# Logits and slot sums behind the v matmuls, one load in the first cycle, and two weight conversions moved into the attention

## The chip, the cores and the metric

The program runs on one core of a Trainium2 chip. A core has five engines with an instruction queue each: TensorE (PE in the profile) multiplies matrices into PSUM, VectorE (DVE), ScalarE (ACT) and GpSimd (POOL) do elementwise work, and SyncE (SP) issues the DMAs here. Each queue runs in order; a wait at its head holds everything behind it. The metric is the device time of one execution in microseconds (us).

## The reference

Attention in chunks of 64 feeds a soft mixture of experts, whose output feeds a gated feed-forward stage.

```
scores = scale * q_c @ k_c.T;  attn = softmax(scores);  x = attn @ v_c     # 8 x 8 heads, 576 tokens, chunks of 64
logits = x @ phi                                                           # x: 4608 x 512, phi: 512 x 32
d = softmax(logits, over tokens);  slot_input = d.T @ x                    # 32 slots, 4 for each of 8 experts
slot_out[e] = relu(slot_input[e] @ w1[e]) @ w2[e]                          # w1: 512 x 1024, w2: 1024 x 512
x2 = softmax(logits, over slots) @ slot_out
g = x2 @ w_gate;  out = (g * sigmoid(g) * (x2 @ w_val)) @ w_out            # 1536 wide
```

The weights w_gate, w_val and w_out arrive as float64. [...]

## The kernel before, in words

The order of the instructions on each engine is that of the program text; nothing reorders them.

**Attention.** The 4608 tokens are 36 tiles of 128. A loop of 19 cycles (k = 0 to 18) handles two tiles per cycle, with the steps of different pairs overlapped. In cycle k, with a = k - 1: logits or the slot sum of an earlier group of four tiles (`emit_logits` in cycles with odd a, `emit_si` in those with even a), the v matmuls of pair a (`emit_pv`, L370, then the reciprocals and the x product on DVE, L386 to L393), the transposes of the scores (`emit_pt`, L356, with the exponential on ACT, L358), the scores of the next pair (`emit_scores`, L333, then max and subtraction on DVE, L341 and L343, tile ssb), POOL's spread of the next v tiles (`spread_v`, L323), the transposes of x (`emit_xt`, L406), and in cycles with odd a the transpose of e (`emit_et`, L458, with its copy on ACT, L460). A slot sum (L471) reads e and four tiles of x. The pool of x has four buffers of one pair each, and a slot sum reads the oldest two.

**Loads.** All loads go through SP's queue. Four q/k tiles and four v tiles are in flight in rings (L290, L293). After each step `pump(n)` takes up to n entries from a list of the loads that later stages need: the float64 data of the first gate and value halves (`load_gv0`), scratch space (`alloc_tmp`, no DMA), then the experts' weights, 32 loads of one MB (`load_w`, L88), with the second gate and value halves (`load_gv0` 1) three entries before their end, then the raw float64 chunks. Each entry needs one of 16 slots; in the attention no slot comes free, and from its end four more are there (in the space of the rings).

**Conversions.** A unit of float64 data passes through `conv_a` (ACT L190, DVE L191 and L192), `conv_b` (ACT L199, DVE L200) and `conv_c` (DVE L205, a product on POOL). `conv_step` moves each unit under way one step on and may start the next; `conv_pos` counts finished units. The first four units are the gate and value halves 0 and 1.

**Experts.** Sixteen steps (w1 or w2 of one expert, L626 and L671), n = 0 to 15, are written with pieces of other work between: steps of the softmax over slots (`emit_c1` on DVE and ACT, `emit_c2` with L709 on PE, at the positions `C_AT`) and conversion steps at the positions `CV_AT`. The last w2 is followed by the scaled slot outputs and the feed-forward stage, which fills the second half of the program.

Of the kernel before, what the change touches and what calls it, by code (L numbers as in the profile page):

```python
# [21 lines left out]
NSP = 9  # L22
RESV = 6
R0 = 7.4
CV_AT = (2, 3, 4, 5, 14)
LATE = 3
C_AT = (3, 4, 5, 6, 7, 9, 10, 11, 12)
RATE = 0.38
# [5 lines left out]
def tile_attn_softmoe_swiglu(  # L34
# [18 lines left out]
    NG = NT // 512  # L53
# [92 lines left out]
    def pump(n=99):  # L146
        while n and lq:
            f, *a = lq[-1]
            if slots[0] > (0 if f in (load_w, load_gv0, alloc_tmp) or a[-1] == 0 else min(resv[0], RESV)):
                f(*a, wp)  # L150
                slots[0] -= 1
                owner[f.__name__, tuple(a)] = 0
            elif slots[1] and f is load_w:
                f(*a, wx[0])
                slots[1] -= 1
                owner[f.__name__, tuple(a)] = 1
            else:
                return
            lq.pop()
            n -= 1  # L160
# [93 lines left out]
    def conv_step(start=True):  # L254
        for k, f in (("d", conv_d), ("c", conv_c), ("b", conv_b)):
            if stage[k]:
                f()
        if start and conv_ready():
            conv_a()

    def conv_busy():
        return bool(stage["b"] or stage["c"] or stage["d"])

    def conv_pos():
        n = len(conv_q) + sum(len(x) for x in stage.values())
        return 6 * NSC - n

    def conv_until(n):
        while conv_pos() < n:
            assert conv_busy() or conv_ready()  # L270
            conv_step(6 * NSC - len(conv_q) < n)

    with tc.manual_schedule():
# [89 lines left out]
        def emit_pv(p):  # L363
            xa = ps_x.tile([128, 2, 512], F32, tag="xa", name="xa_ps")
            xb = ps_x.tile([128, 512], F32, tag="xb", name="xb_ps")
            banks = [xa[:, 0], xa[:, 1], xb]
            for n in range(8):
                i, j = 2 * p + n // 4, n % 4
                for cc in range(2):
                    nc.tensor.matmul(  # L370
                        out=banks[n // 3][64 * cc:64 * cc + 64, (n % 3) * 2 * VW:(n % 3 + 1) * 2 * VW],
                        lhsT=pt_t[i][:, j, 64 * cc:64 * cc + 64],
                        rhs=v_bd[i % NV][:, :, cc, j, :],
                        start=True, stop=True,
                    )
                if j == 3:
                    pt_t.pop(i)
                    if i + NV < NTILE:
                        load_v(i + NV)
            x = xp.tile([128, 2, 512], F32, tag="x", name="x_sb")  # L380
            rec = sm.tile([128, 16, 1], F32, tag="rec", name="rec", bufs=2)
            av = xa[:, :, 0:6 * VW].rearrange("p b (h d) -> p b h d", d=VW)
            bv = xb[:, 0:4 * VW].rearrange("p (h d) -> p h d", d=VW)
            ra, rb = rec[:, 0:12].rearrange("p (b h) o -> p b h o", b=2), rec[:, 12:16]
            xv = x.rearrange("p t (h d) -> p (t h) d", d=D)
            nc.vector.tensor_scalar(out=ra, in0=av[:, :, :, D:VW], scalar1=1e-9, scalar2=None, op0=ALU.add)  # L386
            nc.vector.tensor_scalar(out=rb, in0=bv[:, :, D:VW], scalar1=1e-9, scalar2=None, op0=ALU.add)
            nc.vector.reciprocal(out=rec, in_=rec)
            nc.vector.tensor_tensor(
                out=xv[:, 0:12].rearrange("p (b h) d -> p b h d", b=2), in0=av[:, :, :, 0:D],  # L390
                in1=ra.to_broadcast([128, 2, 6, D]), op=ALU.mult,
            )
            nc.vector.tensor_tensor(  # L393
                out=xv[:, 12:16], in0=bv[:, :, 0:D], in1=rb.to_broadcast([128, 4, D]), op=ALU.mult
            )
            x_t[2 * p], x_t[2 * p + 1] = x[:, 0], x[:, 1]
# [3 lines left out]
        def emit_xt(i):  # L400
            xt = xtp.tile([128, 4, 128], F32, tag="xt", name="xt")
            n = 4 if i < NTILE - 1 else 2
            for j0 in range(0, 4, n):
                ps = ps_t.tile([128, 4, 128], F32, tag="t", name="xt_ps")
                for j in range(j0, j0 + n):
                    nc.tensor.transpose(ps[:, j - j0, :], x_t[i][:, j * 128:(j + 1) * 128], ident)  # L406
                if j0 == 0:
                    nc.scalar.activation(out=xt[:, 0:n], in_=ps[:, 0:n], func=ACTF.Copy)  # L408
                else:
                    nc.vector.tensor_copy(out=xt[:, j0:j0 + n], in_=ps[:, 0:n])  # L410
            xt_t[i] = xt
# [55 lines left out]
        def emit_si(g, mid=None):  # L467
            e = e_t.pop(g)
            ps = ps_t.tile([128, 512], F32, tag="t", name="si_ps")
            for jt in range(4):  # L470
                nc.tensor.matmul(  # L471
                    out=ps[32 * jt:32 * jt + 32, :],
                    lhsT=e[:, 32 * jt:32 * jt + 32],
                    rhs=x_t.pop(4 * g + jt),
                    start=True, stop=True,
                    tile_position=(0, 32 * jt),
                )
            if mid:
                mid()
            if g:  # L480
                be = beta_t.pop(g)
                n = DM // 2 if g == NG - 1 else DM
                for o in range(0, DM, n):
                    nc.vector.scalar_tensor_tensor(
                        out=acc[:, o:o + n], in0=acc[:, o:o + n], scalar=be, in1=ps[:, o:o + n],
                        op0=ALU.mult, op1=ALU.add,
                    )
            else:
                nc.vector.tensor_copy(out=acc, in_=ps)
# [43 lines left out]
        NP = NTILE // 2  # L533
        for k in range(NP + 1):
            a = k - 1
            if a >= 3 and a % 2:
                emit_logits((a - 3) // 2)
            elif a >= 4:
                emit_si((a - 4) // 2)
            if a >= 0:  # L540
                emit_pv(a)
            if k < NP:
                emit_pt(2 * k)
                emit_pt(2 * k + 1)
            if k + 1 < NP:
                emit_scores(k + 1)
                spread_v(2 * k + 2)
                spread_v(2 * k + 3)
            if a >= 1:
                emit_xt(2 * a - 2)  # L550
                emit_xt(2 * a - 1)
            if a >= 3 and a % 2:
                emit_et((a - 3) // 2)
            if k == 0:
                pump(4)
            elif k % 4 != 3:
                pump(1)
        emit_si(NG - 2)
        emit_xt(NTILE - 2)
        emit_xt(NTILE - 1)  # L560
        emit_logits(NG - 1)
        pr.close()
        wx[0] = pa.enter_context(tc.tile_pool(name="wx", bufs=NWX, side="right", reuse_waits="tile"))
# [422 lines left out]
```

## Time and profile before

| | us |
|---|---|
| median of 3 runs | 582.43 (581.38 to 583.82) |
| profiled execution | 582.74 |
| its span, first to last instruction | 579.9 |
| PE busy | 533.8 (92%) |
| DVE busy | 409.4 (71%) |
| ACT busy | 262.1 (45%) |
| POOL busy | 253.1 (44%) |
| slot outputs complete (last L671) | 204.3 |

The span is the part of an execution that the trace shows; the rest lies around it. A busy share is a mean over stages. In the trace a row can carry in brackets how long the engine was idle before it and what released it. "GB/s" is what the 16 DMA engines moved, "DMA share" how busy they were, "PEclk" the clock granted to TensorE as a share of the full one.

### The profile page before, as it was taken

The numbers are of one execution on the slowest core, as the hardware profiler recorded it, in microseconds if no ns is written. First come the engines' busy times: TensorE is split into PE (matmuls) and PEld (weight loads), VectorE is DVE, ScalarE is ACT, GpSimd is POOL, SyncE is SP. The second block draws the span as 40 slices with busy tenths as digits, with TensorE's granted clock in tenths as the row PEclk, the third lists the DMA queues.
The fourth block names the chain that finished last, engine by engine and source line by source line (L and its number), as shares of the span: only waits on it lengthen the run. The fifth ranks groups of instructions, "written<-read, shape, count | busy, mean of one in ns | idle before, by whom it ended". The sixth has DMA issues, their size and how long they took to land.

```text
span 579.9 us, 11070 instructions
## 1 busy us (share of the span) xinstructions
PE 533.8 (92%) x4405; PEld 416.6 (72%) x4405; DVE 409.4 (71%) x679; ACT 262.1 (45%) x508; POOL 253.1 (44%) x252
## 2 busy tenths in 40 slices
PE   7599999998972977999999999999999999999997
PEld 6477777775421465888888887887888788888885
DVE  5557777774643579998888887997989763443464
ACT  1233333334323466766666555554645443333331
POOL 3133424331010226566656665764666463434432
PEclk9889999999995998999999999999999999999999
DMA  8999999976999930010120222024000000032245
GB/s 325 400 393 364 320 360 347 359 255 229 338 387 381 393 113 1 5 68 6 69 73 1 72 73 73 1 73 145 1 1 0 2 1 1 5 122 91 73 173 189
DMA packets 37970, 91.09 MB, mean 157 GB/s; under 512 B 3104, under 2 KB 5152, under 8 KB 37920
## 3 DMA queue, kind: packets, MB, share of 16 engines
q1 hardware_dynamic: 37920, 90.40, 43.0%
q8 instruction: 34, 0.56, 0.4%
q14 instruction: 16, 0.13, 0.1%
HBM read 80.95 MB, written 9.44 MB: 156 GB/s over the span
## 4 chain that ended last, share of the span: by engine, by line
PE 78%; DMA 8%; DVE 6%; ACT 4%; issue 1%; POOL 1%; SPq 1%; DVEq 0%; ACTq 0%; POOLq 0%
PE o L867 17%; PE o L868 16%; PE o L869 16%; PE xa_ps L370 4%; PE v_ps L823 4%; PE g_ps L823 4%; DMA vbd<-in_v_dram 4%; ACT xt L408 3%; PE pt_ps L356 3%; PE s_ps L333 3%; DMA raw<-in_moe_w_gate_dram 2%; DMA raw<-in_moe_w_val_dram 2%; PE xt_ps L406 2%; PE lt_ps L424 2%; PE si_ps L471 2%; PE gg_ps L804 2%
## 5 line engine op out<-in xcount | busy, mean ns | idle before, releaser
L836 POOL TENSOR_TENSOR lo_sb<-s_sb,hi_sb 128x512 fp32r<-128x512 f32 x106 | 140.4, 1325 | 134.1 <-ACT hi_sb L835 130.7
L867 PE MATMUL o<-whl,hi_sb 128*128 128x512 f32 x428 | 168.0, 393 | 2.5 <-DVE part L876 2.5
L869 PE MATMUL o<-whl,lo_sb 128*128 128x512 f32 x428 | 167.4, 391 | 0.5 <-POOL lo_sb L836 0.5
L868 PE MATMUL o<-whl,hi_sb 128*128 128x512 f32 x428 | 167.3, 391 | 0.0
L826 ACT ACTIVATE s_sb<-g_ps 128x512 f32<-128x512 f32 (+1 forms) x110 | 64.7, 590 | 154.3 <-PE g_ps L823 152.1
L827 DVE TENSOR_TENSOR s_sb<-s_sb,v_ps 128x512 f32<-128x512 f32 (+1 forms) x110 | 74.0, 674 | 77.9 <-ACT s_sb L826 76.5
L867 PEld LDWEIGHTS o<-whl,hi_sb 128*128 128x128 f32 x428 | 80.7, 188 | 22.0 <-DVE part L876 4.5
L869 PEld LDWEIGHTS o<-whl,lo_sb 128*128 128x128 f32 x428 | 80.7, 188 | 17.9 <-POOL lo_sb L836 0.9
L868 PEld LDWEIGHTS o<-whl,hi_sb 128*128 128x128 f32 x428 | 80.7, 189 | 16.3
L835 ACT ACTIVATE hi_sb<-s_sb 128x512 fp32r<-128x512 f32 (+1 forms) x110 | 67.6, 616 | 0.8 <-DVE s_sb L827 0.8
L323 POOL COPY vbd<-vbd 64x520 f32<-64x520 f32 x36 | 22.2, 616 | 84.3 <-DMA vbd<-in_v_dram 76.1
L880 DVE TENSOR_TENSOR part<-part,o 128x512 f32<-128x512 f32 x92 | 57.1, 678 | 2.6 <-PE o L869 2.6
L218 POOL TENSOR_TENSOR mt<-mt,ex 128x512 f32<-128x512 f32 x32 | 39.5, 1234 | 30.8 <-PE g_ps L823 15.1
L205 DVE SCALAR_TENSOR_TENSOR ex<-raw,ex 128x512 uint16<-128x512 uint16 x32 | 47.7, 1491 | 0.1
L358 ACT ACTIVATE pt<-pt_ps 128x512 f32<-128x512 f32 x36 | 19.5, 595 | 58.9 <-PE pt_ps L356 58.9
L823 PE MATMUL v_ps<-c_t,g_st 128*128 128x512 f32 (+1 forms) x110 | 42.9, 393 | 3.1 <-ACT s_sb L826 2.5
L823 PE MATMUL g_ps<-c_t,g_st 128*128 128x512 f32 (+1 forms) x110 | 42.5, 389 | 0.2 <-DVE g_st L787 0.2
L200 DVE SCALAR_TENSOR_TENSOR mt<-mt,raw 128x512 f32<-128x512 f32 x32 | 34.6, 1082 | 0.0
L370 PE MATMUL xa_ps<-vbd,pt 128*64 128x130 f32 x432 | 29.2, 286 | 5.3 <-POOL vbd L324 5.3
L370 PEld LDWEIGHTS xa_ps<-vbd,pt 128*64 128x64 f32 x432 | 24.7, 140 | 13.1 <-POOL vbd L324 5.5
L192 DVE TENSOR_SCALAR mt<-raw 128x512 int32<-128x512 int32 x32 | 32.8, 1026 | 0.0
L341 DVE TENSOR_REDUCE m<-s_ps 128x16 f32<-128x1024 f32 x18 | 22.0, 1225 | 13.0 <-PE s_ps L333 13.0
(138 smaller groups left out, 677.3 us busy)
## 6 DMA issues: line engine op xcount, KB each, us to landing
qk<-in_qk_dram SPq DMA_DIRECT2D x36, 512.0 KB, 6.3
w1t<-in_moe_w_dram SPq DMA_DIRECT2D x16, 1024.0 KB, 8.9
w2t<-in_moe_w_dram SPq DMA_DIRECT2D x15, 1024.0 KB, 11.7
vbd<-in_v_dram SPq DMA_DIRECT2D x36, 260.0 KB, 5.6
out_dram<-part SPq DMA_DIRECT2D x36, 256.0 KB, 2.1
raw<-in_moe_w_out_dram SPq DMA_DIRECT2D x6, 1024.0 KB, 5.0
raw<-in_moe_w_gate_dram SPq DMA_DIRECT2D x5, 1024.0 KB, 5.3
raw<-in_moe_w_val_dram SPq DMA_DIRECT2D x5, 1024.0 KB, 6.5
```

What stands on the lines that cost most here:

```text
L205: nc.vector.scalar_tensor_tensor(out=ex, in0=hh, scalar=0x8000, in1=ex, op0=ALU.bitwise_and, op1=ALU.bitwise_or)
L218: nc.gpsimd.tensor_tensor(out=m, in0=m, in1=p, op=ALU.mult)
L370: nc.tensor.matmul(out=banks[n // 3][64 * cc:64 * cc + 64, (n % 3) * 2 * VW:(n % 3 + 1) * 2 * VW], lhsT=pt_t[i][:, j, 64 * cc:64 * cc + 64 ...
L823: nc.tensor.matmul(out=ps[:, k], lhsT=g_st[:, c, gi, ff:ff + 128], rhs=c_blk(b)[:, k], start=True, stop=True)
L826: nc.scalar.activation(out=s[:, k], in_=gp[:, k], func=ACTF.Silu)
L827: nc.vector.tensor_tensor(out=s[:, k], in0=s[:, k], in1=vp[:, k], op=ALU.mult)
L835: nc.scalar.activation(out=hi[:, k], in_=s[:, k], func=ACTF.Copy)
L836: eng.tensor_tensor(out=lo[:, k], in0=s[:, k], in1=hi[:, k].bitcast(F32), op=ALU.subtract)
L867: nc.tensor.matmul(out=a, lhsT=hi[:, ts], rhs=w_hi, start=first, stop=False)
L868: nc.tensor.matmul(out=a, lhsT=hi[:, ts], rhs=w_lo, start=False, stop=False)
L869: nc.tensor.matmul(out=a, lhsT=lo[:, ts], rhs=w_hi, start=False, stop=last)
L880: nc.vector.tensor_tensor(out=p[:, t], in0=p[:, t], in1=a, op=ALU.add)
```

## The change

It edits four places: the list `CV_AT`, the place of `emit_pv` in the cycle, the number of loads in the first cycle with a conversion step at the end of each cycle, and the order at the end of the attention.

```diff
-CV_AT = (2, 3, 4, 5, 14)
+CV_AT = (14,)
...
             a = k - 1
+            if a >= 0:
+                emit_pv(a)
             if a >= 3 and a % 2:
                 emit_logits((a - 3) // 2)
             elif a >= 4:
                 emit_si((a - 4) // 2)
-            if a >= 0:
-                emit_pv(a)
             if k < NP:
...
             if a >= 3 and a % 2:
                 emit_et((a - 3) // 2)
-            if k == 0:
-                pump(4)
-            elif k % 4 != 3:
+            if k == 0 or k % 4 != 3:
                 pump(1)
-        emit_si(NG - 2)
+            conv_step(k >= 4 and conv_pos() < 2 and not conv_busy())
+        conv_until(2)
         emit_xt(NTILE - 2)
         emit_xt(NTILE - 1)
+        emit_si(NG - 2)
         emit_logits(NG - 1)
```

The units of the first gate and value halves are now converted in cycles 4 to 9; when the second is done, two slots come free in the attention. The list of loads gives one entry instead of four in the first cycle, so 10 expert loads stand ahead of the last v loads in SP's queue, where 13 stood.

The SP queue in the first cycles, as a piece of the difference (qk and vbd with numbers are the ring's tiles; w1t is an expert's weights):

```order
 L115 DMA raw<-in_moe_w_val_dram 128x4x256
-L88 DMA w1t<-in_moe_w_dram 128x2x1024 x2
 L293 DMA vbd_101<-in_v_dram 128x520
 L293 DMA vbd_102<-in_v_dram 128x520
 L290 DMA qk_97<-in_qk_dram 128x1024
 L290 DMA qk_98<-in_qk_dram 128x1024
-L88 DMA w1t<-in_moe_w_dram 128x2x1024
 L293 DMA vbd_103<-in_v_dram 128x520
 L293 DMA vbd_104<-in_v_dram 128x520
```

Three expert loads leave the places ahead of the third and fourth pair of v loads.

PE around a slot sum in the middle of the attention, before (xa_ps and xb_ps are the v matmuls, pt_ps the transposed scores, s_ps the scores, xt_ps the transposed x, si_ps the slot sum):

```order
L406 MATMUL xt_ps<-ident,x_sb 128x128 x8
L458 MATMUL e_ps<-ident,et 128x128
L471 MATMUL si_ps<-x_sb,e 32x512 x4
L370 MATMUL xa_ps<-vbd_101,pt 64x130 x8
L370 MATMUL xa_ps<-vbd_102,pt 64x130 x4
L370 MATMUL xb_ps<-vbd_102,pt 64x130 x4
L356 MATMUL pt_ps<-ident,ssb 128x128 x8
```

The same place in the changed kernel:

```order
L406 MATMUL xt_ps<-ident,x_sb 128x128 x8
L458 MATMUL e_ps<-ident,et 128x128
L370 MATMUL xa_ps<-vbd_101,pt 64x130 x8
L370 MATMUL xa_ps<-vbd_102,pt 64x130 x4
L370 MATMUL xb_ps<-vbd_102,pt 64x130 x4
L471 MATMUL si_ps<-x_sb,e 32x512 x4
L356 MATMUL pt_ps<-ident,ssb 128x128 x8
```

The three rows of v matmuls moved between the transpose of e and the slot sum that reads it. The logits moved in the same way in the cycles with odd a.

DVE in the experts before, around the start of the third unit (cst ends one step of the softmax over slots, cm begins the next, tmp and raw are a unit's data; the brackets name the engines or DMA lanes waited for):

```order
L702 TENSOR_TENSOR cst<-cs,chi 128x4x32 [waits DVE_49]
L205 SCALAR_TENSOR_TENSOR tmp<-raw,tmp 128x512
L191 TENSOR_SCALAR tmp<-raw 128x512 [waits DMAHW0_49,PE_49]
L192 TENSOR_SCALAR tmp<-raw 128x512
L686 TENSOR_REDUCE cm<-c_ps 128x4 [waits PE_49]
L688 TENSOR_TENSOR cs<-c_ps,cm 128x128 [waits DVE_49]
```

The start of the third unit in the changed kernel, on the same engine:

```order
L702 TENSOR_TENSOR cst<-cs,chi 128x4x32 [waits DVE_49]
L657 TENSOR_SCALAR ht_2344<-ht_ps 128x4x2x4 [waits PE_49]
L657 TENSOR_SCALAR ht_2345<-ht_ps 128x4x2x4
L657 TENSOR_SCALAR ht_2346<-ht_ps 128x4x2x4
L657 TENSOR_SCALAR ht_2347<-ht_ps 128x4x2x4
L191 TENSOR_SCALAR tmp<-raw 128x512 [waits DMAHW7_49,DMAHW0_49]
L192 TENSOR_SCALAR tmp<-raw 128x512
L200 SCALAR_TENSOR_TENSOR tmp<-tmp,raw 128x512 [waits DVE_49,Activation_49]
```

The third unit moved behind the last step of the softmax (cst) and the last ht of the experts. Four rows of softmax steps that stood behind it now stand ahead of it.

## Rows read from the trace of the kernel before

**Rows 1.** Stages: length; busy us of PE, PEld, DVE, ACT, POOL; PEclk; DMA share; GB/s.

```profile
20.00:40.00 20.00, 13.67 (x251) 11.68 (x243) 8.29 (x17) 4.41 (x11) 4.46 (x8) 0.83 1.03 404
40.00:120.00 80.00, 74.72 (x1536) 58.86 (x1538) 60.21 (x108) 31.11 (x74) 26.84 (x48) 1.00 0.97 349
120.00:140.00 20.00, 18.17 (x284) 13.59 (x277) 11.75 (x28) 7.93 (x22) 4.46 (x8) 1.00 0.56 184
...
150.00:190.00 40.00, 26.14 (x202) 9.58 (x195) 20.58 (x81) 12.99 (x29) 3.58 (x8) 0.83 1.04 383
```

**Rows 2.** PE's timeline, 16 to 41 us: start, length, instruction, [idle before, releaser].

```profile
22.03 1.09 PE L406 MATMUL xt_ps<-ident,x_sb 128*128 128x128 f32 x8
28.41 2.87 PE L370 MATMUL xa_ps<-vbd,pt 128*64 128x130 f32 x24 [5.28 <-POOL vbd L324]
...
33.47 1.16 PE L333 MATMUL s_ps<-qk 64*64 64x64 f32 x64
...
35.58 1.87 PE L424 MATMUL lt_ps<-xt,phi_sb 128*32 128x128 f32 x32
37.38 1.55 PE L370 MATMUL xa_ps<-vbd,pt 128*64 128x130 f32 x24
...
40.33 0.87 PE L333 MATMUL s_ps<-qk 64*64 64x64 f32 x44
```

**Rows 3.** POOL's timeline of the first cycles.

```profile
27.16 0.61 POOL L323 COPY vbd<-vbd 64x520 f32<-64x520 f32 x1 [13.66 <-DMA vbd<-in_v_dram]
```

**Rows 4.** SP's timeline of the first cycles: issue, length, load.

```profile
12.07 1.01 SPq L88 DMA_DIRECT2D w1t<-in_moe_w_dram  x2
13.19 3.43 SPq L293 DMA_DIRECT2D vbd<-in_v_dram  x2
```

**Rows 5.** PE's timeline, one slot sum in the steady attention.

```profile
85.12 1.07 PE L471 MATMUL si_ps<-x_sb,e 128*32 128x512 f32 x8 [0.80 <-ACT e L460]
...
88.05 1.10 PE L356 MATMUL pt_ps<-ident,ssb 128*128 128x128 f32 x8
```

**Rows 6.** PE's groups, 40 to 133 us: instruction, count, busy, mean ns, idle before, releaser.

```profile
L471 PE MATMUL si_ps<-x_sb,e 128*32 128x512 f32 x56 | 7.5, 605 | 5.6 <-ACT e L460 5.6
```

**Rows 7.** PE's timeline from the end of the attention to the slot outputs.

```profile
137.60 1.07 PE L471 MATMUL si_ps<-x_sb,e 128*32 128x512 f32 x8 [0.86 <-ACT e L460]
...
161.22 0.66 PE L709 MATMUL ct_ps<-ident,cst 128*128 128x128 f32 x4
...
164.47 1.92 PE L671 MATMUL so_ps<-w2t,ht 128*32 128x512 f32 x16
...
184.59 1.12 PE L709 MATMUL ct_ps<-ident,cst 128*128 128x128 f32 x4 [13.07 <-ACT cst L699]
...
190.32 1.92 PE L671 MATMUL so_ps<-w2t,ht 128*32 128x512 f32 x16
...
202.84 1.49 PE L671 MATMUL so_ps<-w2t,ht 128*32 128x512 f32 x20
```

**Rows 8.** DVE's timeline, conversion steps in the experts.

```profile
180.97 0.43 DVE L191 TENSOR_SCALAR tmp<-raw 128x512 uint16<-128x512 uint16 x1 [13.80 <-DMA raw<-in_moe_w_gate_dram]
...
198.66 1.65 DVE L205 SCALAR_TENSOR_TENSOR tmp<-raw,tmp 128x512 uint16<-128x512 uint16 x1
```

**Rows 9.** DVE's timeline in the same cycle as rows 5.

```profile
84.52 1.22 DVE L343 TENSOR_TENSOR ssb<-s_ps,m 128x1024 f32<-128x1024 f32 x1
```

**Rows 10.** SP's timeline, the last two v loads.

```profile
121.99 1.20 SPq L293 DMA_DIRECT2D vbd<-in_v_dram  x2
```

**Rows 11.** DMA issues of the whole program: load, count, KB each, median us to landing.

```profile
w1t<-in_moe_w_dram SPq DMA_DIRECT2D x16, 1024.0 KB, 8.9
...
vbd<-in_v_dram SPq DMA_DIRECT2D x36, 260.0 KB, 5.6
...
raw<-in_moe_w_gate_dram SPq DMA_DIRECT2D x2, 512.0 KB, 11.4
```

**Rows 12.** DMA issues between 179 and 180.3 us: load, count, KB each, us to landing.

```profile
w2t<-in_moe_w_dram SPq DMA_DIRECT2D x2, 512.0 KB, 11.3
```

## The prediction

> **What bounds the kernel now.** I read the busy time by stage first, then TensorE's timeline for idle time over half a microsecond, then the engine that each such gap waits for, and last the DMA queue. In this program TensorE (PE) sets the end: from 260 us on it has hardly a gap, so time can only be won before that, and a stage counts for what PE idles or runs slowly in it. Four things stand out before 205 us.
>
> First, a gap of 5.28 us ahead of the v matmuls that start at 28.41, and a granted clock of 0.83 between 20 and 40 us [rows 1, 2]. The clock's two levels are 1.2 and 2.4 GHz; after that gap the same work runs at the lower one. Its releaser is POOL's spread of a v tile, which began at 27.16 after waiting 13.66 us for a DMA [rows 3]. That DMA was issued at 13.19, right behind two expert loads issued from 12.07 [rows 4].
>
> Second, every slot sum (L471) waits 0.80 us for the copy of e on ACT: seven times between 40 and 133 us, 5.6 us together, and once more with 0.86 us at 137.60 [rows 5, 6, 7].
>
> Third, PE stands still for 13.07 us before 184.59, in the experts [rows 7]. The releaser named is ACT's cst, but the reader should look one engine further: DVE sat idle for 13.80 us until 180.97, waiting for the load of a raw gate half, and went on with line 191 [rows 8]. A conversion of the third float64 unit stands in the in-order queues of DVE and ACT ahead of the softmax work that PE needs.
>
> Fourth, the DMA engines: 404 GB/s between 20 and 40 us, 349 in the steady attention, only 184 between 120 and 140, and 383 in the experts [rows 1]. The low stretch is where the sixteen weight slots are full.
>
> **The change part by part.** The sum is made against the profiled execution, 582.74 us, of which the span is 579.9; the median of the runs shown is 582.43, so a difference made here can be taken off either.
>
> *One load in the first cycle.* The SP queue loses two loads of 1024 KB between the raw v half and the v load that PE waits for, and a third before the next pair of v loads. Two loads are 2.10 MB; at the 404 GB/s of that stretch they take 5.2 us. Without them the spread would begin near 22.0 instead of 27.16, and the v matmuls, which start 1.25 us after it [rows 2, 3], near 23.2. PE is done with the xt transposes of the cycle at 23.12 [rows 2], so the gap closes to about 0.1. Without the gap I also expect no lower clock: from the start of the v matmuls to that of the scores it was 5.06 us (28.41 to 33.47) and in the next cycle 2.95 (37.38 to 40.33) [rows 2], 2.1 us more. Term A is 5.2 + 2.1 = 7.3 us. Bounds: 4 if the queue brings the v tile 3 us later than I think, 8 if nothing is late.
>
> *Logits and slot sums behind the v matmuls.* PE then has the v matmuls (1.9 us) to do while ACT copies e. The 0.80 us goes seven times. At the end of the attention the e copy now stands ahead of two xt transposes instead of the slot sum, so the 0.86 goes too, but the last e follows its logits with only one pair of transposes between; I leave 0.4 us for that. Term B is 5.6 + 0.86 - 0.4 = 6.1 us. What is late next: the x product on DVE (L389) gets a wait for the slot sum, since x has four buffers and the slot sum reads the one that is overwritten. That wait holds DVE about 1 us, the length of the slot sum [rows 5], and behind it stand the accumulation, the max and the subtraction (ssb). Now ssb is done at 85.74 and PE wants it at 88.05 [rows 5, 9]: 2.3 us of slack, of which 0.8 was the wait that goes. 1.5 us is left, so I charge nothing. Bounds: a gain of 6.5, or a loss of 1 us in each of the eight slot sums, which leaves a loss of 2.
>
> *Two units converted in the attention.* Each unit adds four DVE, two ACT and one POOL instruction, one or two per engine and cycle from the fifth cycle on. DVE is busy 60.2 of 80 us there [rows 1]. The slowest of these instructions took 1.65 us beside a POOL instruction [rows 8], about the slack that is left. I take 0, for they stand behind ssb of their cycle and so delay only the next reciprocals, which have their own slack; the upper end is four two-input instructions at 1.65, 6.6 us, if nothing covers them. A gain is excluded: their absence in the experts is counted below.
>
> On this the Trainium skill says (GPSIMD Engine Reference, section Specifications) that GpSimd's SBUF interfaces are shared with VectorE and contend with DVE instructions that have two SBUF inputs. The 1.65 us agrees with it. By that rule alone each L200 and L205 would meet POOL's spreads, and the sum would come out up to 6.6 us later, the end already named.
>
> *Four conversion steps taken out of the experts.* With only position 14 left, the third unit's first instruction stands behind all softmax and ht work on DVE, as the order shows. Nothing of PE is behind it but the end of the stage. So the 13.07 us gap goes, and with it the slow clock after it: ct, one w2 expert, ct took 5.73 us (184.59 to 190.32) where the same at full clock took 3.25 (161.22 to 164.47) [rows 7], 2.5 us. Term D is 15.6 us. It is the largest term, and the one whose place is taken by something else first.
>
> *What is late next: the expert weights.* On PE alone the last slot output, now at 204.33 (202.84 + 1.49) [rows 7], would come at 204.33 - 7.3 - 6.1 - 15.6 = 175.3. The DMA queue has a say. The last v loads were issued from 121.99 [rows 10]. They come earlier by 7.3, by six slot-sum waits (4.8) and by one group of logits (1.87) [rows 2] that no longer stands ahead: 108.0. Ten expert loads are asked for before that (the order shows thirteen before the change), so 22 loads and one gate and value pair of 512 KB each follow: 23.1 + 1.05 MB. In flight at that moment: the median v load lands after 5.6 us [rows 11], at 349 GB/s some 2.0 MB, an estimate. 26.1 MB at 385 GB/s take 67.8 us: the last weights land at 175.8. The six loads that follow the last v load need no PE: three of them took their turn from the cycles, three find free slots, so the stretch of 184 GB/s fills up. Before, the last halves were issued after 179 and took 11.3 us [rows 12], so they landed near 191, and PE with its 15 us of stall never met them. Now it does: 175.8 plus the matmuls of the last half (0.7, half of the 1.49) is 176.5, later than 175.3. The gain is 204.33 - 176.5 = 27.8 us. The stage behind it begins 27.8 us earlier and is unchanged: its first conversion needs a raw load that follows the last weights by 2.7 us (1.05 MB at 385) and lands near 178.5, 2 us after the slot output; since ACT, PE and DVE pass the slot outputs on first, I take it as just in time.
>
> 582.74 - 27.8 = 555.0 us.
>
> **The rivals.**
>
> *B, the queue goes more slowly.* For it: 349 GB/s is what the steady attention got. Against it: there the cycles asked for no more (share 0.97), and 383 to 404 were had where loads stood in line [rows 1]. At 349 the 26.1 MB take 74.8 us, the last weights land at 182.8 and the slot output comes at 183.5: 582.74 - 20.8 = 562 us. To it belongs the first raw load coming late by up to 3 us.
>
> The Trainium skill (DMA: Bandwidth & Descriptors, section Specifications) gives about 358 GB/s as the limit of HBM for one core. The trace disagrees: 404 over 20 us. By 358 the 26.1 MB would take 72.9 us and the time would be 560, inside this rival.
>
> *C, DVE is the bound of the attention.* The conversions, x waiting for the slot sum and POOL's spreads add up to more than the slack in the cycles that convert. Price 4 to 8 us on the attention; half of it hides behind the DMA queue, which is late anyway. 558 to 564 us.
>
> *D, the wait moves instead of going.* The third unit's load stands four loads from the end of the weights (3.1 MB, 8 us), so it lands near 167.7, and its chain on ACT, DVE and POOL has some 8 us to the end of the stage. If the conversions end only after the last slot output by as much as PE gained, only A and B stay: 582.74 - 13.4 = 569, and up to 576 with C beside it. Against it: in this trace the two last units ran from the ht work to 200.3 (198.66 + 1.65) [rows 8] while PE was still at its matmuls.
>
> *E, slower.* One mechanism: x waits for the slot sum, the slot sum for e, e for the logits of the cycle before, and these now for later v matmuls, so that DVE and PE run in lockstep with x's four buffers. It decides from the point where e comes more than the 1.9 us of v matmuls late: each further microsecond is paid in eight cycles. To be slower than before by 0.5% it must cost (27.8 + 2.9)/8 = 3.8 us a slot sum, 586 us. Against it: e is 0.80 us late now [rows 5].
>
> **How the numbers follow.** Forecast 0.68 (its own range 550 to 560), B 0.13, C 0.07, D 0.06, E 0.03; 0.03 for under 549, with every bound at its good end and the queue at 404 GB/s (64.6 us, 3 us less). The range 549 to 566 takes in B and C and leaves D, E and the low end out. 0.5% is 2.9 us, about what a measurement of this kernel can tell from no change: faster 0.93, within it 0.03, slower 0.04.
>
> **What would show it.** A: no gap over 1 us ahead of the third v matmuls and full clock from 20 to 40 us. B: L471 with no idle from ACT between 30 and 120 us, and a pair of cycles of 13.1 us instead of 13.9. Conversions: L191, L200 and L205 in the attention with ssb still before PE's demand. D: no DVE wait for a raw gate load before the last c_ps; PE dense from the first expert on, or waiting for w2t at the end, which is the meeting with the queue. Slot output near 176.5. I am wrong if the experts still hold a gap over 5 us, if PE waits for a v spread in the steady cycles, or if the stage after the experts takes longer than it did.

## The result and the profile after

| | before | after |
|---|---|---|
| median (range), us | 583.0 (581.4 to 583.8, 4 executions) | 552.49 (552.1 to 555.1, 4) |
| profiled execution, us | 582.74 | 552.5 |
| its span, us | 579.9 | 550.6 |
| end of the attention's last logits (L424), us | 141.3 | 126.8 |
| slot outputs complete (last L671), us | 204.3 | 175.1 |
| from there to the end of the span, us | 375.6 | 375.5 |
| mean clock granted to TensorE | 0.979 | 1.000 |

The changed kernel takes 0.9489 of the time before (95% interval 0.9453 to 0.9526). 555.0 was forecast; 552.5 is inside the forecast's own range of 550 to 560. The last row but one says where to look: everything was won before the slot outputs (29.2 us of 30.2; 0.9 us of the rest lies outside the span), and the stage behind them only starts earlier. Of the 29.2, 14.5 us were won up to the end of the attention and 14.7 in the experts.

The stages of the changed kernel, in the columns of [rows 1]:

```profile
20.00:40.00 20.00, 18.88 (x408) 15.53 (x410) 15.14 (x28) 8.47 (x19) 9.29 (x16) 1.00 0.98 374
40.00:105.00 65.00, 63.03 (x1377) 51.07 (x1367) 53.56 (x103) 27.67 (x69) 24.66 (x42) 1.00 1.00 376
...
120.00:150.00 30.00, 26.41 (x261) 12.34 (x249) 17.65 (x77) 10.12 (x28) 2.31 (x11) 1.00 1.04 394
150.00:180.00 30.00, 27.36 (x230) 12.86 (x229) 16.41 (x53) 15.01 (x32) 3.08 (x5) 1.00 1.05 384
```

Full clock from 20 to 40 us (it was 0.83), and no stretch up to 180 us in which the DMA queue runs low: between 120 and 150 us it moves 394 GB/s, where 120 to 140 had 184.

TensorE's timeline of the first cycles, as in [rows 2], start and length in us:

```profile
22.50 1.09 PE L406 MATMUL xt_ps<-ident,x_sb 128*128 128x128 f32 x8
23.53 1.55 PE L370 MATMUL xa_ps<-vbd,pt 128*64 128x130 f32 x24
...
26.47 1.58 PE L333 MATMUL s_ps<-qk 64*64 64x64 f32 x64
...
30.93 1.08 PE L424 MATMUL lt_ps<-xt,phi_sb 128*32 128x128 f32 x32
```

The v matmuls follow the transposes without a gap. The scores behind them start at 26.47 instead of 33.47. POOL's spread of the v tile, the releaser of [rows 3], now begins at 21.47:

```profile
21.47 0.61 POOL L323 COPY vbd<-vbd 64x520 f32<-64x520 f32 x1 [7.18 <-DMA vbd<-in_v_dram]
```

TensorE's timeline in the steady attention, against [rows 5]; one pair of cycles from the v matmuls at 99.88 to those at 112.39:

```profile
99.88 1.55 PE L370 MATMUL xa_ps<-vbd,pt 128*64 128x130 f32 x24
...
101.80 1.07 PE L471 MATMUL si_ps<-x_sb,e 128*32 128x512 f32 x8
102.80 1.09 PE L356 MATMUL pt_ps<-ident,ssb 128*128 128x128 f32 x8
...
112.39 1.55 PE L370 MATMUL xa_ps<-vbd,pt 128*64 128x130 f32 x24
```

TensorE's groups, 40 to 120 us, against [rows 6] (busy, mean ns, idle before):

```profile
L471 PE MATMUL si_ps<-x_sb,e 128*32 128x512 f32 x48 | 6.4, 605 | 0.0
```

The slot sum has no idle time left (5.6 us before, 0.80 each). A pair of cycles takes 12.5 us; from one slot sum to the next it was 13.9.

VectorE in the same cycle, against [rows 9], and one conversion step:

```profile
44.20 0.68 DVE L200 SCALAR_TENSOR_TENSOR tmp<-tmp,raw 128x512 f32<-128x512 f32 x1
...
99.87 1.22 DVE L343 TENSOR_TENSOR ssb<-s_ps,m 128x1024 f32<-128x1024 f32 x1
...
102.90 0.96 DVE L389 TENSOR_TENSOR x_sb<-xa_ps,rec 128x768 f32<-128x768 f32 x1 [0.54 <-PE si_ps L471]
```

ssb is done at 101.09 and TensorE wants it at 102.80. The new wait of x for the slot sum is there (0.54 us) and reaches nobody.

TensorE from the end of the attention to the slot outputs, against [rows 7]:

```profile
123.00 0.33 PE L458 MATMUL e_ps<-ident,et 128*128 128x128 f32 x1 [1.19 <-ACT lt_all L449]
...
125.78 1.06 PE L424 MATMUL lt_ps<-xt,phi_sb 128*32 128x128 f32 x32
...
132.73 1.92 PE L626 MATMUL h_ps<-w1t,si_m 128*32 128x512 f32 x16 [0.34 <-DVE si_m L604]
...
168.75 1.06 PE L671 MATMUL so_ps<-w2t,ht 128*32 128x512 f32 x8 [0.84 <-DMA w2t<-in_moe_w_dram]
...
173.65 1.49 PE L671 MATMUL so_ps<-w2t,ht 128*32 128x512 f32 x20
```

The 13.07 us stall is gone. Two short waits for w2 take its place at the very end, this one and one of 0.66 at 171.57. The conversions, against [rows 8], now wait at 164.53 for the raw gate half and nobody waits for them:

```profile
164.53 0.43 DVE L191 TENSOR_SCALAR tmp<-raw 128x512 uint16<-128x512 uint16 x1 [1.73 <-DMA raw<-in_moe_w_gate_dram]
...
168.94 1.65 DVE L205 SCALAR_TENSOR_TENSOR tmp<-raw,tmp 128x512 uint16<-128x512 uint16 x1
```

The chain that ended last, 150 to 180 us (start, length, what), shows what bounds the end of the experts:

```profile
159.43 0.28 PE so_ps L671
159.71 11.72 DMA w2t<-in_moe_w_dram
171.43 0.14 issue
171.57 1.06 PE so_ps L671 x8
```

The view begins the load at 159.71, where a w2 matmul ends; it lands 11.72 us later, behind some 4.5 MB of loads in flight (an estimate: 11.72 us at 384 GB/s), and TensorE waits for it. TensorE and the DMA queue meet here. Which of the two sets the issue is settled by a run below, and it is the queue.

### The profile page after: what moved, and what is told of

It reads as the page before. It is cut to its first block, busy times and chain, and to the rows that moved or that the text cites. A ratio compares the mean times of both kernels' runs of the same rounds, so it can differ in the third digit from the quotient of the medians.

```text
span 550.6 us, 11078 instructions
## 1 busy us (share of the span) xinstructions
PE 523.5 (95%) x4405; PEld 410.8 (75%) x4405; DVE 407.1 (74%) x679; ACT 260.8 (47%) x508; POOL 253.3 (46%) x252
## 4 chain that ended last, share of the span: by engine, by line
PE 83%; DVE 7%; DMA 4%; ACT 2%; issue 2%; POOL 1%; SPq 0%; ACTq 0%; DVEq 0%; POOLq 0%
PE o L867 17%; PE o L869 17%; PE o L868 17%; PE v_ps L823 4%; PE g_ps L823 4%; PE xa_ps L370 4%; PE xt_ps L406 3%; PE h_ps L626 3%; PE s_ps L333 3%; PE pt_ps L356 2%; DMA w2t<-in_moe_w_dram 2%; PE gg_ps L804 2%; PE si_ps L471 2%; PE so_ps L671 2%; DMA qk<-in_qk_dram 1%
## 5 line engine op out<-in xcount | busy, mean ns | idle before, releaser
L205 DVE SCALAR_TENSOR_TENSOR ex<-raw,ex 128x512 uint16<-128x512 uint16 x32 | 47.7, 1492 | 0.1
L200 DVE SCALAR_TENSOR_TENSOR mt<-mt,raw 128x512 f32<-128x512 f32 x32 | 34.6, 1081 | 0.0
L370 PE MATMUL xa_ps<-vbd,pt 128*64 128x130 f32 x432 | 27.9, 277 | 0.0
L823 PEld LDWEIGHTS v_ps<-c_t,g_st 128*128 128x128 f32 x110 | 20.5, 188 | 8.7 <-ACT s_sb L826 3.9
```

The costliest lines, as they stand in the source:

```text
L205: nc.vector.scalar_tensor_tensor(out=ex, in0=hh, scalar=0x8000, in1=ex, op0=ALU.bitwise_and, op1=ALU.bitwise_or)
L370: nc.tensor.matmul(out=banks[n // 3][64 * cc:64 * cc + 64, (n % 3) * 2 * VW:(n % 3 + 1) * 2 * VW], lhsT=pt_t[i][:, j, 64 * cc:64 * cc + 64 ...
L823: nc.tensor.matmul(out=ps[:, k], lhsT=g_st[:, c, gi, ff:ff + 128], rhs=c_blk(b)[:, k], start=True, stop=True)
```

## The experiments

The change has four parts: one load in the first cycle, the order of the attention, the conversion steps out of the experts, and the two units converted in the attention instead (a conversion rebuilds float64 weights in float32). Each was taken back from the changed kernel, and the first three were also put into the kernel before alone; the fourth never was. Among these runs come a part taken apart further, tests of the cover of two edits, and one run that bears on a miss.

**The order taken back** (v matmuls behind the logits and slot sums, and the old end of the attention).

```diff
             a = k - 1
-            if a >= 0:
-                emit_pv(a)
             if a >= 3 and a % 2:
                 emit_logits((a - 3) // 2)
             elif a >= 4:
                 emit_si((a - 4) // 2)
+            if a >= 0:
+                emit_pv(a)
...
+        emit_si(NG - 2)
         emit_xt(NTILE - 2)
         emit_xt(NTILE - 1)
-        emit_si(NG - 2)
```

> The changed kernel with the old order of the attention (logits and slot sums ahead of the v matmuls, the old tail). Theory M (each slot sum waited 0.8 us for e and each group of logits some 0.8 us for xt, the latter hidden inside long matmul rows; now both hide; behind the attention 1.5 us of waits for expert weights take up the first of any loss): the attention ends 12.5 us later, the slot outputs 11 us later, 563.5 us. Rival R1 (the sizes of the prediction: only the wait for e, 6.1 us): 557 us. Rival R2 (the weight queue alone sets the slot outputs, the order of PE is worth nothing): 552.5 us.

Measured: 562.5 us (561.2 to 564.3), ratio to before 0.9644 [0.9615, 0.9673], against 0.9489 of the changed kernel: 9.0 us more. TensorE's timeline of this run:

```profile
92.76 1.07 PE L471 MATMUL si_ps<-x_sb,e 128*32 128x512 f32 x8 [0.80 <-ACT e L460]
...
98.82 1.87 PE L424 MATMUL lt_ps<-xt,phi_sb 128*32 128x128 f32 x32
...
106.67 1.06 PE L471 MATMUL si_ps<-x_sb,e 128*32 128x512 f32 x8 [0.80 <-ACT e L460]
```

The wait is back, the pair is 13.9 us again, and the logits take 1.87 instead of 1.08. So a pair costs 1.4 us more, and only 0.8 of it is the wait that the rows of TensorE name. The attention ends 8.2 us later, where M had 12.5, and the slot outputs come 9.0 us later, where it had 11. So R1 and R2 are excluded, but M was too large; its 563.5 comes near partly because the first 16 matmuls of the experts ran at the lower clock in the profiled execution (3.49 us, 1.92 in the changed kernel).

**Only the slot sums ahead of the v matmuls again** (the logits and the end stay as changed).

```diff
+            if a >= 4 and a % 2 == 0:
+                emit_si((a - 4) // 2)
             if a >= 0:
                 emit_pv(a)
             if a >= 3 and a % 2:
                 emit_logits((a - 3) // 2)
-            elif a >= 4:
-                emit_si((a - 4) // 2)
```

> The changed kernel with only the slot sums back ahead of the v matmuls; the logits stay behind them. M: the wait for e comes back seven times (5.6 us), logits stay at 1.1 us a group; 1.5 us hides in waits for weights: 556.6 us, about 6.5 us less than with both put back. R1: 557 us, and the same time as with both put back. R2: 552.5 us.

Measured: 558.1 us (557.3 to 558.4), 0.9564 [0.9539, 0.9588]. TensorE's groups, 40 to 125 us:

```profile
L424 PE MATMUL lt_ps<-xt,phi_sb 128*32 128x128 f32 x200 | 6.9, 276 | 0.0
...
L471 PE MATMUL si_ps<-x_sb,e 128*32 128x512 f32 x48 | 6.4, 605 | 4.9 <-ACT e L460 4.9
```

By the ratios this part costs 4.4 us of the 9.0, where the waits of all seven slot sums add up to 5.7 (six of them stand in this row). M expected 4.1, and 6.5 more with both put back; R1 expected nothing more. It is 4.7 more. The logits keep their short form: their part is separate.

**The loads taken back.**

```diff
-            if k == 0 or k % 4 != 3:
+            if k == 0:
+                pump(4)
+            elif k % 4 != 3:
                 pump(1)
```

> The changed kernel with four entries of the load list in the first cycle again. M: the gap ahead of the third v matmuls (5.3 us) and the slow clock behind it (2.1) come back, attention ends 7 us later, 1.5 of it hides in waits for weights: 558 us. R2 (the bytes in the queue are the same and the queue sets the end): 552.5 us.

Measured: 557.8 us (557.1 to 560.0), 0.9568 [0.9539, 0.9597]. The gap ahead of the third v matmuls returns with 3.22 us (5.3 was expected; the matmuls start 4.8 us later than in the changed kernel), the lower clock with it (0.83 from 20 to 40 us), in TensorE's timeline:

```profile
28.32 2.87 PE L370 MATMUL xa_ps<-vbd,pt 128*64 128x130 f32 x24 [3.22 <-POOL vbd L324]
```

In this execution, the slowest of the four, the slot outputs come 6.8 us later, near term A; the ratios give 4.6.

**The conversion steps taken back** (a start of the third unit in the experts again; the first two units stay in the attention).

```diff
-CV_AT = (14,)
+CV_AT = (5, 14)
```

> The changed kernel with a conversion step at position 5 of the experts again, where the third unit stood before. M: DVE waits for the gate half, which lands near 164 us; PE stalls from about 154, and goes on as it did before, slot outputs 23.4 us behind the landing, near 188 instead of 175: 565 us. Rival R2 (the queue alone; the stall only fills time in which the weights were not there): 554 us at most.

Measured: 567.1 us (566.6 to 568.0), 0.9723 [0.9701, 0.9745]. TensorE's timeline:

```profile
169.00 1.12 PE L709 MATMUL ct_ps<-ident,cst 128*128 128x128 f32 x4 [11.24 <-ACT cst L699]
170.26 3.64 PE L671 MATMUL so_ps<-w2t,ht 128*32 128x512 f32 x16
```

VectorE's timeline, the instruction that everything behind it waits for:

```profile
165.38 0.43 DVE L191 TENSOR_SCALAR tmp<-raw 128x512 uint16<-128x512 uint16 x1 [13.56 <-DMA raw<-in_moe_w_gate_dram]
```

The stall is back with the lower clock behind it (3.64 for 16 matmuls that take 1.92), and the releaser two engines further on is the raw load. Slot outputs at 188.5.

**Three parts alone, each put into the kernel before.** The edits are those of the change; for the conversions it is `CV_AT = (14,)` alone, with no unit converted in the attention.

> The kernel before with the new order of the attention alone. M: attention 12.5 us shorter; all that follows (queue refilled from the end of the attention, stall until the gate half has landed) moves with it: 570 us. R1 (only the wait for e): 576.5 us. R2 (the queue alone): 582 us.

> The kernel before with one entry of the load list in the first cycle, alone. M: early gap and slow clock gone, 7 us, and what follows moves with it: 575.5 us. R2 (the loads that leave the first cycle have to be made later): 582 us.

> The kernel before with conversion steps at position 14 alone, so that all four units are converted at the end of the experts. M: the stall of 13 us goes, then PE meets the last weights, which land near 191 us as before: slot outputs near 192, a gain of 12.5 instead of 15.6 us: 570 us. Rival D (the wait only moves to the end, four units of conversions behind the gate half): 578 us or more.

Measured: the order alone 577.8 us (three executions from 575.5 to 579.1; a fourth of 1049 us is left out of the ratio), 0.9901 [0.9878, 0.9924], a miss of 7.8 us (6.6 by the ratio). R1's 576.5 lies inside its interval, but not R1's mechanism: the logits take 1.08 us in this run, as M has it. The load alone 575.9 (574.1 to 578.4), 0.9902 [0.9871, 0.9933]. The conversions alone 570.9 (569.8 to 572.5), 0.9815 [0.9792, 0.9839]. In the last, the stall is gone and TensorE waits for w2 instead:

```profile
185.59 1.06 PE L671 MATMUL so_ps<-w2t,ht 128*32 128x512 f32 x8 [2.80 <-DMA w2t<-in_moe_w_dram]
```

Gains by the ratios, times 582.4 us:

| parts in the kernel | gain, us |
|---|---|
| load | 5.7 |
| order | 5.8 |
| steps out of the experts | 10.8 |
| load, order, units in the attention | 16.1 |
| load, steps, units | 20.7 |
| order, steps, units | 25.2 |
| load, order, steps (the run without conversions in the attention, below) | 24.4 |
| all four | 29.8 |

The three parts alone make 22.3 together, and the run with just these three gives 24.4. Either figure has an uncertainty of about 2.6 us by the intervals, so the two can't be told apart: that a part is worth more beside another is not shown by these sums. Taken out of the changed kernel, the load is worth 4.6 us, the order 9.0, the steps 13.6 and the units 5.4, each to within 2.5 to 3.4. That is no more than alone for the load and some 3 us more for the order and the steps, at the edge of the intervals.

**Why the order alone gave so little.** Its trace: the attention ends only 5.3 us earlier than before, where 12.5 was expected (the order taken back showed 8.2), and the stall in the experts ends 2.4 us earlier (182.23 against 184.59 in [rows 7]). Clock and DMA rates of this run (columns of [rows 1]):

```profile
120.00:130.00 10.00, 8.01 (x106) 5.91 (x106) 5.02 (x15) 2.46 (x6) 0.00 (x0) 1.00 0.29 101
...
140.00:150.00 10.00, 9.66 (x61) 4.25 (x63) 3.75 (x21) 1.11 (x3) 0.43 (x3) 0.70 0.40 131
```

VectorE's timeline of this run:

```profile
178.60 0.43 DVE L191 TENSOR_SCALAR tmp<-raw 128x512 uint16<-128x512 uint16 x1 [14.28 <-DMA raw<-in_moe_w_gate_dram]
```

The raw half, deep in the queue, lands 2.4 us earlier, and the stall waits for it. The expectation of the next run puts the loss between 5.3 and 2.4 down to the queue that ran dry. The trace points to the clock instead. It fell at the attention's end (the last logits took 1.85 us) and was still low in the first expert, whose 16 matmuls took 1.92 us in the kernel before (the three executions had mean clocks of 0.969 to 0.971, those of the kernel before beside them 0.976 to 0.979). TensorE's timeline of this run:

```profile
142.79 3.51 PE L626 MATMUL h_ps<-w1t,si_m 128*32 128x512 f32 x16 [0.34 <-DVE si_m L604]
```

SP's timeline shows the loads that need the first expert's slots, first in this run and then in the kernel before:

```profile
146.38 18.70 SPq L88 DMA_DIRECT2D w2t<-in_moe_w_dram  x9
```

```profile
149.20 18.30 SPq L88 DMA_DIRECT2D w2t<-in_moe_w_dram  x9
```

They begin 2.8 us earlier, so 2.5 of the 5.3 us were gone before the queue filled again, and behind that only 0.4 was lost. If the stall waits for the load, it must shrink when this load stands nearer to the front. The test moves it four entries up in the kernel with the order alone:

```diff
-LATE = 3
+LATE = 7
```

> The kernel before with the new order alone, and the loads of the second gate and value halves four entries (4 MB) earlier in the list of loads; no instruction of PE, DVE, ACT or POOL moves. The order alone gave 577.8 us, where 570 was expected. Theory M: the order's gain at the end of the attention (5.3 us there by its trace) was eaten in the experts, since the stall ends with the landing of the raw gate half, which the queue brought only 2.3 us earlier because it ran dry between 120 and 150 us. With that load 4 x 1.05 MB / 385 GB/s = 10.9 us earlier, the stall of 13.55 us shrinks to under 3 us, the slot output comes near 190 instead of 201.8, met there by the last weights, and the time is 566 us (564 to 568), below the 570.9 of the conversions moved alone. Rival R: the place of the conversion instructions in the queues of DVE and ACT costs by itself, whenever their data lands: the stall stays over 8 us and the time is 574 us or more.

Measured: 568.5 us (565.9 to 569.7), 0.9766 [0.9728, 0.9804], 7.9 us less than without by the ratios. TensorE's timeline:

```profile
166.03 1.12 PE L709 MATMUL ct_ps<-ident,cst 128*128 128x128 f32 x4 [7.44 <-ACT cst L699]
...
188.90 1.49 PE L671 MATMUL so_ps<-w2t,ht 128*32 128x512 f32 x20
```

VectorE's timeline:

```profile
162.40 0.43 DVE L191 TENSOR_SCALAR tmp<-raw 128x512 uint16<-128x512 uint16 x1 [6.17 <-DMA raw<-in_moe_w_gate_dram]
```

The raw half lands 16 us earlier: 5.0 of that because this execution kept its full clock and the first expert's slots were loaded from 141.39 on, the other 11.2 by the four entries (10.9 was expected). The slot outputs come at 190.4 (near 190 was expected), and the rival's 574 is excluded; the time lies just above the expected 564 to 568. The stall shrank to 7.44, not under 3, no wait for the last weights followed it, and the expectation was wrong in saying that nothing moves on VectorE: a unit starts as soon as its load is listed, so its first two instructions moved ahead of one softmax step and TensorE met the wait two w1 steps earlier. That the wait is for the load is shown. That a dry queue ate the order's gain is not: the earlier load was not run in the kernel before without the order, so what it gives there by itself is not known.

**No conversions in the attention** (all four units at the end of the experts).

```diff
-            conv_step(k >= 4 and conv_pos() < 2 and not conv_busy())
-        conv_until(2)
```

> The changed kernel without conversions in the attention: all four units at the end of the experts, and no slots freed in the attention. M: the attention is at most 1 us shorter (the conversions there cost nothing that matters), but two loads fewer can start before the rings are free, so the queue runs dry for some 5 us around 130: last weights and slot outputs 5 us later, 557.5 us. Rival C (the conversions hold up PE in the attention): 548 to 551 us. Rival (conversions and slots both without effect): 552.5 us.

Measured: 557.9 us (553.7 to 560.1), 0.9581 [0.9535, 0.9626]. Taking them out of the attention does not shorten it: the last logits start at 126.44, 0.7 us later than in the changed kernel. Four w1 loads that SP had issued by 123.4 us there (116.56 + 6.84) are out only by 137.5 here (120.12 + 17.35), since two slots are missing, and TensorE waits for w2 at the end. TensorE's timeline:

```profile
175.03 1.09 PE L669 MATMUL so_ps<-w2t,ht 128*32 128x512 f32 x8 [3.13 <-DMA w2t<-in_moe_w_dram]
```

How much of the 5.4 us is due to the slots stays open. This execution, the slowest of the four, ran at the lower clock at the attention's end (the last logits took 1.89 us), and the first 16 matmuls of the experts ended 4.0 us later than in the changed kernel (138.64 against 134.65); the DMA engines stood nearly idle from about 134.5 to 138.7, when the slots of the first expert were loaded again. The execution with the highest mean clock (0.997) took 553.7 us, a time that the changed kernel has too. The 557.5 that was expected was met, but not by the slots alone as far as this trace shows.

**The cover at the end: three runs.** The first puts the last transpose of e, which waits 1.19 us in the changed kernel, between the two x transposes behind it. The second leaves out one 1 MB load (the second half of the last expert's w1; its matmuls read the first half twice), the third does both.

```diff
-            if a >= 3 and a % 2:
+            if a >= 3 and a % 2 and k < NP:
                 emit_et((a - 3) // 2)
...
         emit_xt(NTILE - 2)
+        emit_et(NG - 2)
         emit_xt(NTILE - 1)
```

```diff
-        lq += [(load_w, i, e, 0), (load_w, i, e, 1)]
+        lq += [(load_w, i, e, 0)] + ([(load_w, i, e, 1)] if (i, e) != (0, E - 1) else [])
```

> The changed kernel with the last transpose of e but one behind one more xt transpose, so that PE does not wait 1.2 us for it at the end of the attention. M (the weight queue sets the slot outputs): attention 1.2 us shorter, slot outputs unmoved, 552.5 us. Rival (PE sets them): 551.3 us.

> The changed kernel with one expert load of 1 MB left out (the second half of w1 of expert 7; its matmuls read the first half again, so that part of the output is another number). M: the queue is 2.7 us shorter, PE's two waits for weights (1.5 us) go: 551.0 us. Rival (PE sets the slot outputs): 552.5 us.

> Both: the transpose of e moved and the load of 1 MB left out. M: with the queue out of the way the 1.2 us of the attention count: 549.8 us. Rival (the parts add up as they did alone, 0 for the first): 551.0 us.

Measured: 553.7 us (552.7 to 557.9, 6 executions), 551.6 (550.2 to 554.4, 5) and 554.3 (552.5 to 555.5, 5). The times overlap with each other and with those of the changed kernel and settle nothing; the third missed its 549.8. The trace of the first does tell:

```profile
124.98 1.06 PE L424 MATMUL lt_ps<-xt,phi_sb 128*32 128x128 f32 x32
...
168.80 1.07 PE L672 MATMUL so_ps<-w2t,ht 128*32 128x512 f32 x8 [1.68 <-DMA w2t<-in_moe_w_dram]
```

The attention ends 0.8 us earlier, the wait for w2 is 0.84 us longer, and the next step behind the slot outputs starts at 175.83 (175.79 in the changed kernel). The 0.8 us became a weight wait, as expected of a stage that ends with the queue. It also settles the chain in the section on the result: TensorE is 0.8 us earlier here at the w2 matmuls that stand ahead of the load, and yet the load begins at 159.69 (159.71 there) and lands within 0.1 us of the same time. So the queue set it, and TensorE did not. In the second no wait for w2 is left, but TensorE ran at the lower clock for some microseconds in the first expert; in the third at the end of the attention. What those two would have given at an equal clock stays open. None of the three is clearly faster than the changed kernel.

## Why the prediction was right, point by point

**One load in the first cycle: right.** 7.3 us forecast, 7.0 by the start of the scores behind the third v matmuls (33.47 to 26.47). The gap closed and the clock stayed at its full level, as forecast; that the lower clock follows the gap is shown by the run with the loads taken back, where both return.

**Logits and slot sums behind the v matmuls: right in kind, term B too small.** 6.1 us forecast; the attention's 14.5 less the 7.0 leaves 7.5, and taking the order back costs 8.2 there. The step that failed is reading the logits' 1.87 us in [rows 2] as work. TensorE's weight loads in the kernel before show that it waits inside that row, twice, for ACT's copy of xt:

```profile
91.19 0.14 PEld L424 LDWEIGHTS lt_ps<-xt,phi_sb 128*32 128x32 f32 x4 [0.17 <-issue]
91.50 0.14 PEld L424 LDWEIGHTS lt_ps<-xt,phi_sb 128*32 128x32 f32 x2 [0.17 <-ACT xt L408]
91.99 0.79 PEld L424 LDWEIGHTS lt_ps<-xt,phi_sb 128*32 128x32 f32 x26 [0.35 <-ACT xt L408]
```

In the changed kernel the same 32 follow each other:

```profile
95.35 0.81 PEld L424 LDWEIGHTS lt_ps<-xt,phi_sb 128*32 128x32 f32 x32 [0.17 <-DVE rec L386]
```

So the v matmuls cover two waits per pair, not one, and a pair in which nothing is converted won 1.4 us (12.5 for 13.9) where 0.8 was forecast. Not every pair did: from the first logits to the seventh the six pairs won 6.5 us, the first only 0.2 and the three with conversions 1.0 to 1.3. The Trainium skill (Perfetto Trace Analysis, section Identifying the Most-Contended Engine) says that the busy share of the matmul row is not a good measure of how close a kernel is to its roofline, and names the busy share of the weight loads beside another measure to use instead. It says this of shares, not of a wait inside one row; here too the weight loads tell more: 1.87 against 1.08 us on the one row, 1.07 against 0.81 of loads with the waits named on the other. At the end of the attention 0.4 us was left for the last e; the waits there are 1.19, 0.16 and 0.26 us, so that part was too good by about 1.2. The total does not test term B: with 1.5 us of waits for weights at the end, a microsecond more or less in the attention would hardly have moved the slot outputs.

**Conversions in the attention at no cost: nearly right.** They lie behind ssb, and ssb keeps 1.7 us of slack in the cycle shown. But the cost is not nothing: TensorE waits 0.23, 0.31 and 0.45 us for ACT (the copy lt_all) in the cycles that convert, and the three pairs from the logits at 44.61 to those at 82.84 take 38.2 us, where the run without conversions there takes 37.5. The bound of 6.6 us came from the 1.65 us row; in the attention the two L200 took 0.68 each and the two L205 0.68 and 0.89. On the port rule that was weighed: the L205 of 0.89 began beside one of POOL's spreads (69.30, 0.62 long), the slow row of 1.65 stands where it stood, at the end of the experts (168.94), beside POOL's product (168.50, 1.54 long). Rival C's 4 to 8 us did not come.

**Conversion steps out of the experts: right.** The stall is gone and so is the slow clock behind it. From the first w1 matmul to the slot outputs it was 57.1 us (147.22 to 204.33) and is 42.4: 14.7 us, against 15.6 less the 1.2 that was given to the queue, 14.4. Alone the part gives 10.8, since the queue ends it there with a wait of 2.8; taken back it costs 13.6 (both by the ratios). Rival D, a wait that moves, didn't come: the conversions end at 170.6, ahead of the slot outputs.

**The meeting with the DMA queue: right in place, forecast 1.4 us too late.** The first weights behind the last v loads were issued at 108.39 (108.0 forecast for the last v loads) and the slot outputs came at 175.14 (176.5). It moved 376 to 394 GB/s from 40 to 180 us in the stretches above, but for the one left out there (363 from 105 to 120); from 108 to 171.5 it was 384, where 385 was taken. Rival B's 349 was not a limit, as argued. Of the 358 GB/s that was weighed beside it: the traces exceed it here too, and the Trainium skill itself (HBM Reference, section Specifications (TRN2)) reads that figure as the share when both cores of a pair stream, so it should not have been set against one core alone. The prediction let the queue run on without TensorE, and the run with the last transpose of e moved bears that out: there TensorE was 0.8 us earlier and the last loads were not.

**Rival E, lockstep: wrong.** x waits 0.54 us for the slot sum, TensorE never waits for that x, and the slot sums in the steady cycles wait for nothing.

## What to carry to other kernels

Where a stage ends with whichever comes last of a load, a conversion and the matmuls, price a gain up front by following it to the next meeting: 0.8 us won at the end of the attention became a longer wait for weights, and the conversion steps alone gave 10.8 us, where the stall and its slow clock had cost 15.6, with a wait of 2.8 for w2 in the stall's place. Read the granted clock of both traces before naming a cause: with the order alone it took 2.5 of the 5.3 us that the attention had won. Before calling parts more than their sum, run the same parts together: 22.3 and 24.4 us can't be told apart here, and the 29.8 holds a fourth part. Read TensorE's weight-load row beside its matmul row before calling a long matmul group work.

## What the runs showed of the hardware

The clock granted to TensorE behind the end of the attention differed between runs with the same short waits ahead. In the changed kernel the first 16 matmuls of the experts took 1.92 us (the row at 132.73 above); with one load left out, TensorE's waits from the attention's end had the same lengths (1.19, 0.16, 0.26, 0.95 and 0.37 us), and behind them the clock fell: the six short matmuls ahead of the experts (tile warm) took 1.40 instead of 0.94 us, and then came this row of TensorE's timeline:

```profile
134.81 3.64 PE L626 MATMUL h_ps<-w1t,si_m 128*32 128x512 f32 x16 [0.34 <-DVE si_m L604]
```

The clock's levels are 1.2 and 2.4 GHz; 3.64 for 1.92 is the lower one, and it costs 1.7 us in this row alone. The order taken back and the conversions taken back had it at this place too, the last logits of the order alone and of the run without conversions a little earlier. Four executions of the changed kernel had mean clocks from 0.991 to 1.000 and ran from 552.1 to 555.1 us. What decides it the runs don't show. Three microseconds lie between those four, so an edit worth less can't be told here by a few times alone.
